# FFN products of 3584 tokens by Strassen's algorithm, with weight sums made once and weights streamed from DRAM

## The chip, the cores and the metric

The kernel runs on one core of a Trainium2 chip. A core has TensorE (matmul), VectorE, ScalarE and GpSimd, which compute on SBUF and PSUM, and SyncE, which here issues the DMAs. The metric is the time on the device in microseconds, as the median of three runs.

## The reference

Block-causal attention (8 batches of 8 heads, 576 positions, 64 wide) gives x; a gated projection with a 5-tap convolution follows; and its result goes through the part that the change touches:

```python
X = np.fft.fft(x, axis=1); X = np.fft.fft(X, axis=2)
u = x + np.real(X).astype(np.float32)
mu = np.mean(u, axis=-1, keepdims=True)
var = np.mean((u - mu) ** 2, axis=-1, keepdims=True)
un = (u - mu) / np.sqrt(var + 1e-06)
ch = np.maximum(un @ w_ch1, 0.0) @ w_ch2      # 512 -> 2048 -> 512
return (u + ch).astype(np.float32)
```

There are 8 x 576 = 4608 tokens. The weights arrive as float64.

## The kernel before

Every float32 product is made of three matmuls on parts of the operands: a high part (the value rounded to the format fp32r) and a low part (what is left): high by high, high by low and low by high. A high part is a copy on ScalarE, a low part a subtraction on VectorE.

phase1() makes attention, gate and the Fourier mix and stores u to DRAM (u_d, one tile for each batch). It ends near 690 us of the trace. XF holds the factors of a head pair; the loads L496 bring some of them back from DRAM. In its last batch first_weights() decodes the weights of hidden blocks 0 and 1 in quarters: a raw load (L891), a decode on ScalarE and VectorE, the high part (L895) and the low part (L896, tiles KP and KL among them).

phase2() is the FFN. The 4608 tokens go in NG = 9 groups of T = 512. A group runs over 16 blocks f of 128 hidden units: 12 matmuls of 512 columns into the PSUM tile psh (L1185 to L1187), relu as the high part hh on ScalarE (L1190), the low part hl on VectorE (L1191), and one block later 12 matmuls into the four sums o (L1204 to L1206). A group is 384 matmuls. At its end VectorE multiplies o by r = 1/sqrt(var) (L1213), GpSimd adds u (L1215; VectorE in the last group), and the rows are stored (L1216). The norm of the next group (norm(), L1139 to L1159) runs in between; its means are matmuls with a matrix of ones (average(), L1121 and L1122). From group 2 on GpSimd makes parts of it. Group 0 also decodes the weights: load_raw (L1082, two DMAs of 0.5 MB for a block, called five blocks ahead, three used up front) and load_w (decode L71 to L82, high part W at L1092, low part W at L1093). The weights of all 16 blocks then stay in SBUF.

A scheduler of the tile framework fixes each engine's order before the run; an engine takes its instructions in that order and waits for semaphores. All DMAs of phase 2 stand in SP's one queue. They take eight semaphores in turn (DMAHW0 to 7), and each waits for the DMA eight before it.

Of the kernel before, what the change touches and what calls it, by code (L numbers as in the profile page):

```python
# [17 lines left out]
def kernel(  # L18
# [13 lines left out]
    nc = tc.nc  # L32
# [61 lines left out]

    cst = ctx.enter_context(tc.tile_pool(name="cst", bufs=1))
# [9 lines left out]
    W1H, W1L, W2H, W2L = ([None] * NF for _ in range(4))  # L105

    def w_places(f, t):
        W1H[f], W1L[f], W2H[f], W2L[f] = (x[:, 0:D] for x in t)

    def w_sources(f):  # L110
        return ((w_ch1[:, f * P:(f + 1) * P].bitcast(I32).rearrange("(c p) f -> p c f", p=P), W1H[f], W1L[f]),
                (w_ch2[f * P:(f + 1) * P, :].bitcast(I32).rearrange("p (c f) -> p c f", c=4), W2H[f], W2L[f]))
# [4 lines left out]
    def phase1():  # L117
        with ExitStack() as c1:
# [766 lines left out]
            def first_weights(z):  # L885

                src, h, l = w_sources(z // 4)[z // 2 % 2]
                hf = z % 2
                h, l = (t[:, 256 * hf:256 * hf + 256] for t in (h, l))
# [3 lines left out]
                st = QHL.rearrange("p t s -> p (t s)")[:, 256 * (z % 4):256 * (z % 4) + 256].bitcast(F32)  # L893
                Chain(wait, wait, wait, wait, *decode(r, st, True),
                      lambda: nc.scalar.copy(out=h, in_=st),  # L895
# [142 lines left out]
    def phase2():  # L1038
        with ExitStack() as c2:
# [11 lines left out]
            NG = NTOK // T  # L1051
            s3 = sb("s3", 2)
            rp = sb("rp", 1)
# [3 lines left out]
            wp = [sb(f"wp{i}", 1) for i in range(2, NF)]  # L1057
            wh = sb("wh", 1)
            wb = sb("wb", 1)
            ps_o, ps_h, ps_t = psum("ps_o", 1), psum("ps_h", 2), psum("ps_t", 2)  # L1060
# [4 lines left out]
            US = [wa.tile([P, 4, T], F32, name="U0")]  # L1065
            UHS = [wa.tile([P, 4, T], F32R, name="UTH0")]
            ULS = [wa.tile([P, 4, T], F32R, name="UTL0")]
            HH = [wa.tile([P, T], F32R, name=f"hh{i}") for i in range(2)]
            HL = [wa.tile([P, T], F32R, name=f"hl{i}") for i in range(2)]
            US.append(wb.tile([P, 4, T], F32, name="U1"))  # L1070
            ULS.append(wb.tile([P, 4, T], F32R, name="UTL1"))

            RAW = {}

            def load_raw(f):

                if not 1 < f < NF:
                    return
                pool = rp if f in (2, NF - 1) else wp[f] if f < NF - 2 else wh
                RAW[f] = pool.tile([P, 4 * D], I32, tag="w", name="rw")  # L1080
                for z, (src, _, _) in enumerate(w_sources(f)):
                    nc.sync.dma_start(out=RAW[f][:, 2 * D * z:2 * D * z + 2 * D].rearrange("p (c f) -> p c f", c=4),  # L1082
                                      in_=src)

            def load_w(f):
                W = wp[f - 2].tile([P, 4 * D], F32R, tag="w", name=f"W{f}")
                w_places(f, [W[:, D * z:D * z + D] for z in (0, 2, 1, 3)])
                h, l = W[:, 0:2 * D], W[:, 2 * D:4 * D]
                st = s3.tile([P, 2 * D], F32, tag="st", name="st")
                for stage in decode(RAW[f], st):  # L1090
                    stage()
                nc.scalar.copy(out=h, in_=st)  # L1092
                nc.vector.tensor_tensor(out=l, in0=st, in1=h.bitcast(F32), op=ALU.subtract)  # L1093

            U, UTH, UTL, RS = {}, {}, {}, {}

            def load_u(g):
                if g >= NG:
                    return
                U[g] = US[g % 2]  # L1100
                done = 0
                while done < T:
                    b, s = divmod(g * T + done, S)
# [210 lines left out]
```

## Time and profile before

| what | value |
|---|---|
| runs | 1474.63, 1480.74, 1481.87 us, median 1480.74 us |
| profiled execution | 1476.05 us, of which the span is 1474.2 us |
| TensorE, VectorE, ScalarE, GpSimd busy | 1420.3, 815.5, 644.5, 309.7 us |
| phase 1, groups 0 and 1, groups 2 to 8 | to about 690 us, to about 850 us, to the end |

The span is the time between the first and the last record of the profiled execution; 1.85 us lie outside it. Busy times are sums over an engine's instructions. The chain of work that ended last is TensorE's for 73% of the span.

### The profile page before, as it was taken

The page shows a single profiled execution, that of the slowest core. Times are in us where ns is not written, and L with a number is a line of the kernel's source. Part 1 is how long each engine was busy: PE and PEld are TensorE (multiplying, and loading weights), DVE is VectorE, ACT ScalarE, POOL GpSimd, SP SyncE. Part 2 cuts the span into 40 slices and gives each one's busy share as a digit, 9 for nine tenths or more (in the row PEclk, how much of TensorE's full clock was granted, in tenths as well). Part 3 has the DMA queues.
Part 4 walks back from the last instruction along what each step waited for, and adds up shares of the span by engine and source line. Part 5 has one row for each costly group of instructions (what it writes and reads, how often), then busy time and mean ns, then how long its engine had stood idle before and what let it go on. Part 6 is the DMA issues. An engine that isn't in the chain of part 4 may idle for free.

```text
span 1474.2 us, 22875 instructions
## 1 busy us (share of the span) xinstructions
PE 1420.3 (96%) x8543; PEld 1205.5 (82%) x8543; DVE 815.5 (55%) x1618; ACT 644.5 (44%) x1627; POOL 309.7 (21%) x254
## 2 busy tenths in 40 slices
PE   5798999999999999999999999999999999999998
PEld 3576888999989898888788888888888888888887
DVE  5777797979797979898983222322232223222212
ACT  5687777777777777734532112121121212112110
POOL 3423232323232323222011011111011111011100
PEclk9799999999999999999999999999999999999999
DMA  7567565656565656353500010100101010010000
GB/s 207 151 161 212 152 179 145 173 148 176 146 177 147 174 150 167 99 175 114 204 29 29 0 57 1 57 0 17 42 0 57 1 53 5 0 58 1 29 0 29
DMA packets 121611, 137.22 MB, mean 93 GB/s; under 512 B 23567, under 2 KB 91421, under 8 KB 121501
## 3 DMA queue, kind: packets, MB, share of 16 engines
q1 hardware_dynamic: 120960, 135.63, 32.2%
q8 instruction: 67, 1.10, 0.3%
q14 instruction: 44, 0.35, 0.1%
q10 hardware_dynamic: 540, 0.14, 0.0%
HBM read 70.57 MB, written 19.01 MB: 61 GB/s over the span
## 4 chain that ended last, share of the span: by engine, by line
PE 73%; DVE 10%; issue 6%; DMA 4%; POOL 3%; ACT 3%; SPq 1%; DVEq 0%; ACTq 0%; POOLq 0%
PE psh L1187 8%; PE psh L1185 8%; PE psh L1186 8%; PE o L1206 8%; PE o L1204 8%; PE o L1205 8%; PE av L605 4%; PE pt L577 4%; DVE gate L632 2%; PE sc L417 2%; POOL XA L838 2%; PE sc L418 2%; PE psx L181 1%; DVE mx L449 1%; PE psx L182 1%
## 5 line engine op out<-in xcount | busy, mean ns | idle before, releaser
L1191 DVE SCALAR_TENSOR_TENSOR hl<-psh,hh 128x512 fp32r<-128x512 f32 x144 | 99.4, 690 | 398.4 <-ACT hh L1190 398.3
L1190 ACT ACTIVATE hh<-psh 128x512 fp32r<-128x512 f32 x144 | 86.1, 598 | 500.2 <-PE psh L1187 500.0
L1187 PE MATMUL psh<-UTH,W 128*128 128x512 f32 x504 | 196.2, 389 | 1.2 <-DVE W L1093 1.2
L1185 PE MATMUL psh<-UTH,W 128*128 128x512 f32 x504 | 196.2, 389 | 1.1 <-ACT W L1092 1.1
L1206 PE MATMUL o<-hl,W 128*128 128x512 f32 x504 | 196.2, 390 | 0.0
L1186 PE MATMUL psh<-UTL,W 128*128 128x512 f32 x504 | 196.1, 389 | 0.0
L1204 PE MATMUL o<-hh,W 128*128 128x512 f32 x504 | 196.1, 389 | 0.0
L1205 PE MATMUL o<-hh,W 128*128 128x512 f32 x504 | 196.0, 389 | 0.0
L463 ACT ACTIVATE PB<-sc,mx 128x128 f32<-128x128 f32 (+4 forms) x320 | 167.0, 527 | 52.8 <-DVE mx L449 29.5
L577 PE MATMUL pt<-ident,PB 128*128 128x128 f32 x800 | 141.9, 283 | 15.4 <-ACT PTb L583 8.1
L577 PEld LDWEIGHTS pt<-ident,PB 128*128 128x128 f32 x800 | 101.0, 144 | 32.5 <-ACT PTb L583 14.5
L632 DVE SCALAR_TENSOR_TENSOR gate<-XF,cw,gate 128x575 f32<-128x575 f32 (+3 forms) x128 | 122.2, 955 | 4.5 <-ACT gate L63 3.6
L1187 PEld LDWEIGHTS psh<-UTH,W 128*128 128x128 f32 x504 | 94.6, 188 | 21.3 <-DVE W L1093 1.6
L1215 POOL TENSOR_TENSOR U<-o,U 128x512 f32<-128x512 f32 x32 | 40.3, 1288 | 341.0 <-DVE o L1213 341.0
L1185 PEld LDWEIGHTS psh<-UTH,W 128*128 128x128 f32 x504 | 94.6, 188 | 21.1 <-ACT W L1092 1.5
L1206 PEld LDWEIGHTS o<-hl,W 128*128 128x128 f32 x504 | 94.5, 188 | 20.6 <-DVE hl L1191 1.0
L1204 PEld LDWEIGHTS o<-hh,W 128*128 128x128 f32 x504 | 94.6, 188 | 19.9 <-ACT hh L1190 0.2
L1205 PEld LDWEIGHTS o<-hh,W 128*128 128x128 f32 x504 | 94.6, 188 | 19.8
L1186 PEld LDWEIGHTS psh<-UTL,W 128*128 128x128 f32 x504 | 94.6, 188 | 19.6
L449 DVE TENSOR_REDUCE mx<-sc 128x1 f32<-128x384 f32 (+2 forms) x192 | 104.3, 560 | 4.4 <-PE sc L183 2.7
L417 PE MATMUL sc<-K,QQ 128*128 128x256 f32 (+2 forms) x256 | 87.9, 354 | 13.4 <-DMA QQ<-QHL 12.5
L628 POOL TENSOR_TENSOR XL<-XF,XH 128x576 fp32r<-128x576 f32 x32 | 45.9, 1434 | 249.3 <-ACT XH L57 249.1
(226 smaller groups left out, 3122.0 us busy)
## 6 DMA issues: line engine op xcount, KB each, us to landing
K<-KP SPq DMA_DIRECT2D x128, 144.0 KB, 2.5
QQ<-QHL SPq DMA_DIRECT2D x128, 128.0 KB, 2.5
rw<-in_w_ch SPq DMA_DIRECT2D x28, 512.0 KB, 7.2
VV<-in_v SPq DMA_DIRECT2D x32, 320.0 KB, 3.6
qraw<-in_q SPq DMA_DIRECT2D x32, 288.0 KB, 3.3
kraw<-in_k SPq DMA_DIRECT2D x32, 288.0 KB, 3.3
out<-U SPq DMA_DIRECT2D x36, 256.0 KB, 2.0
QQ<-QHL SPq DMA_DIRECT2D x128, 64.0 KB, 2.4
```

The source lines that it names most:

```text
L417: nc.tensor.matmul(t[:, o:o + w], q[:, 0, m], KK[p][h][:, 0:w], start=True, stop=False)
L449: nc.vector.reduce_max(out=mx[:, j:j + 1], in_=t, axis=AX.X, negate=one)
L463: nc.scalar.activation(out=PB[i][:, k0:k0 + w], in_=t, func=AF.Exp, bias=nm, accum_out=su[:, at + j:at + j + 1])
L577: nc.tensor.transpose(ps[:, j, :], PB[i][:, (j0 + j) * P:(j0 + j + 1) * P], ident)
L632: nc.vector.scalar_tensor_tensor(out=gate[c][:, s:S], in0=XF[:, 0:S - s], scalar=cw[:, c, 4 - s:5 - s], in1=gate[c][:, s:S], op0=ALU.mult, ...
L1185: nc.tensor.matmul(ps, W1H[f][:, c * P:c * P + P], UTH[g][:, c, :], start=(c == 0), stop=False)
L1186: nc.tensor.matmul(ps, W1H[f][:, c * P:c * P + P], UTL[g][:, c, :], start=False, stop=False)
L1187: nc.tensor.matmul(ps, W1L[f][:, c * P:c * P + P], UTH[g][:, c, :], start=False, stop=(c == 3))
L1191: nc.vector.scalar_tensor_tensor(out=l, in0=ps, scalar=0.0, in1=h.bitcast(F32), op0=ALU.max, op1=ALU.subtract)
L1204: nc.tensor.matmul(po[t], W2H[e][:, c], h, start=(e == 0), stop=False)
L1205: nc.tensor.matmul(po[t], W2L[e][:, c], h, start=False, stop=False)
L1206: nc.tensor.matmul(po[t], W2H[e][:, c], l, start=False, stop=(e == NF - 1))
```

## The change

The first NG = 2 groups are computed as before, with layer 2 two blocks behind layer 1 in place of one, in the same PSUM banks under new names. The other 3584 tokens go in NQ = 4 quads of 896 tokens, two halves of N = 448. Each layer of a quad is a product of 2 x 2 half-blocks by Strassen's algorithm in Winograd's form, seven products in place of eight: the order of the products is L1O and L2O, and a step (g, l, p, i) is a quarter of product p, 12 matmuls of 448 columns. A quad has 56 steps.

- Weights: group 0 stores the decoded weights of each block (w_d, 0.52 MB) and the high and low parts of the blocks that products use unchanged (base_d, 0.79 MB), through SP; first_weights and keep_base do so for blocks 0 and 1. combine() runs in group 1: 16 units that load 0.52 MB from w_d, make four sums on VectorE, split them and store 1.05 MB to comb_d. In the quads every two steps take one chunk of 1.05 MB from base_d or comb_d, in a ring of six SBUF tiles.
- Operands: sums() makes sums of blocks of X or of the hidden blocks h on GpSimd (896 elements a row), operand() the high part on ScalarE and the low part on VectorE, LOOK = 3 steps ahead in a ring of four tiles.
- Results: a product of layer 1 lies in two PSUM banks (a ring of three pairs) and is added into h by VectorE (28 additions a quad, two for each quarter of p = 5), then relu on ScalarE. A product of layer 2 is added to the loaded rows of u (y11, y12, y21, y22) or to e by VectorE, e to y by GpSimd; then the rows are stored.
- norm_x() normalises the next quad's X in place, 448 columns at a time, with sums, squares' sums and half of the scaling on GpSimd.

```diff
+    NH = NF // 2
+    w_d = [dram.tile([P, 2 * D], F32, name=f"w_d{f}") for f in range(NF)]
+    base_d = [[dram.tile([3, P, NH // 2 * D], F32, name=f"base_d{i}{z}") for z in range(2)] for i in range(2)]
+    comb_d = [[dram.tile([4, P, NH // 2 * D], F32, name=f"comb_d{i}{z}") for z in range(2)] for i in range(2)]
...
+                      lambda: (nc.sync.dma_start(out=keep, in_=st), nc.scalar.copy(out=h, in_=st)),
...
-            NG = NTOK // T
+            NG = 2
+            N = 448
+            NQ = (NTOK - NG * T) // (2 * N)
...
+                if f < 2:
+                    for y in range(3):
+                        nc.sync.dma_start(out=to[:, y], in_=WQ[f][y + i].bitcast(F32))
+                    return
...
+                nc.sync.dma_start(out=to, in_=WW[f][:, i * D:i * D + 3 * D].bitcast(F32).rearrange("p (s c) -> p s c", c=D))
...
+                nc.sync.dma_start(out=w_d[f], in_=st)
...
+                def load(k):
+                    if k < len(units):
+                        i, j = units[k]
+                        ins[k] = s3.tile([P, 2, D], F32, tag="st", name="ab")
+                        for z in range(2):
+                            nc.sync.dma_start(out=ins[k][:, z, :], in_=w_d[j + NH * z][:, D * i:D * i + D])
...
+                    t = two[0][:, k % 2]
+                    p = at(("H0", "L0")[k % 2], [P, 4, 2, 256], F32R, "packed")
+                    for z, a, b, op in ((0, a21, a22, ALU.add), (1, t[:, 0], a11, ALU.subtract),
+                                        (2, a11, a21, ALU.subtract), (3, a12, t[:, 1], ALU.subtract)):
+                        nc.vector.tensor_tensor(out=t[:, z], in0=a, in1=b, op=op)
+                    load(k + 2)
+                    nc.scalar.copy(out=p[:, :, 0, :], in_=t)
+                    nc.vector.tensor_tensor(out=p[:, :, 1, :], in0=t, in1=p[:, :, 0, :].bitcast(F32), op=ALU.subtract)
+                    z, jj = divmod(j, NH // 2)
+                    nc.sync.dma_start(out=comb_d[i][z][:, :, jj * D:jj * D + D].rearrange("s p c -> p s c"),
+                                      in_=p.bitcast(F32).rearrange("p s y c -> p s (y c)"))
+                    yield
...
+            L1O, L2O = (1, 6, 2, 7, 5, 3, 4), (1, 3, 5, 2, 6, 7, 4)
+            steps = [(g, l, p, i) for g in range(NQ) for l in range(2) for p in (L1O, L2O)[l] for i in range(4)]
...
+            ring_w = [4, 5, 6, 7, 8, 9]
+            ring_o = [10, 11, 12, 13]
...
+                chunk[c] = at(ring_w[c % 6], [P, 4, 2, 256], F32R, "chunk")
+                src = SRC[l, p][z][SLOT[l, p]] if (l, p) in SRC else comb_d[l][z][SLOT[p]]
+                nc.sync.dma_start(out=chunk[c].bitcast(F32).rearrange("p j y c -> p (j y c)"), in_=src)
...
+                        for t in range(4):
+                            (nc.gpsimd if t % 2 else nc.vector).tensor_tensor(
+                                out=u[:, t, :], in0=u[:, t, :], in1=r, op=ALU.mult)
...
+                x, y, z = {5: (b, b, a), 6: (d, d, b), 7: (a, d, a), 4: (c, d, c)}.get(p, (None,) * 3)
+                if x is not None:
+                    nc.gpsimd.tensor_tensor(out=x, in0=y, in1=z, op=ALU.subtract)
...
+                o = at(ring_o[nitem[0] % 4], [P, 2, 2, N], F32R, "o")
+                nitem[0] += 1
+                nc.scalar.copy(out=o[:, 0], in_=x)
+                nc.vector.tensor_tensor(out=o[:, 1], in0=x, in1=o[:, 0].bitcast(F32), op=ALU.subtract)
...
+                if l == 0:
+                    ps = banks[(k + 2) % 3]
...
+                            nc.tensor.matmul(to, wh, o[:, 0, t], start=(t == 0), stop=False)
+                            nc.tensor.matmul(to, wh, o[:, 1, t], start=False, stop=False)
+                            nc.tensor.matmul(to, wl, o[:, 0, t], start=False, stop=(t == 1))
+                    ps = ps[:, :, 0:N]
+                    a, b, c, d = (hb[z][i // 2][:, i % 2 * 2:i % 2 * 2 + 2] for z in range(4))
+                    if p == 1:
+                        nc.scalar.copy(out=a, in_=ps)
+                        return
+                    for to, x in {6: ((b, a),), 2: ((a, a),), 7: ((c, b),), 5: ((d, c), (b, b)), 3: ((b, b),),
+                                  4: ((c, c),)}[p]:
+                        if p == 4:
+                            nc.vector.tensor_tensor(out=to, in0=x, in1=ps, op=ALU.subtract)
+                        else:
+                            nc.vector.tensor_tensor(out=to, in0=ps, in1=x, op=ALU.add)
...
+                        nc.scalar.activation(out=h, in_=h, func=AF.Relu)
...
+                ps = banks[(k // 4 + 2) % 3]
...
+            LOOK = 3
...
-                for f in range(NF + 1):
+                for f in range(NF + 2):
+                    if g == 0 and f == 0:
+                        for e in range(2):
+                            keep_base(e)
                     if g == 0 and f + 2 < NF:
...
-                    if f == (5 if g else NL):
-                        nxt = norm(g + 1)
+                        keep_base(f + 2)
+                    if g == 0 and f == 9:
+                        load_u(1)
+                    if g == 0 and f == NL:
+                        nxt = norm_g(1)
+                    if g and f == 5:
+                        load_x(0)
+                        nxt = norm_x(0)
+                    if g and 7 <= f < 13:
+                        load_chunk(f - 7)
...
+                for _ in mix:
+                    pass
+                if g == NG - 1:
+                    prepare(3)
...
-                    (nc.vector if g == NG - 1 else nc.gpsimd).tensor_tensor(out=x0, in0=x, in1=x0, op=ALU.add)
+                    nc.gpsimd.tensor_tensor(out=x0, in0=x, in1=x0, op=ALU.add)
...
+                n = k % 56
+                if n == 0:
+                    load_x(g + 1)
+                    nxt = norm_x(g + 1)
+                if k % 2 == 0:
+                    load_chunk(k // 2 + 6 - 1) if k else None
+                if l == 0 and n >= 24:
+                    j = k + 12
+                    src[j + 0] = sums(j)
+                if l and 8 <= n - 28 < 20:
+                    j = k + 8
+                    src[j] = sums(j)
+                if n in (20, 22, 24, 26):
+                    load_y(g, (12, 22, 11, 21)[(n - 20) // 2])
+                prepare(k + LOOK)
+                product(k)
+                if l == 0 or n == 27:
+                    next(nxt, None)
+                if l:
+                    next(nxt, None)
```

SP (the queue of DMAs) at the end of phase 1, before; XF1 holds the last head pair's factors, rw raw weights, and DMAHW, DVE and so on name the semaphores waited for:

```order
L891 DMA rw_8614<-in_w_ch2 128x512 [waits DMAHW7_49,DVE_49,Activation_49]
L891 DMA rw_8616<-in_w_ch2 128x512 [waits DMAHW0_49,DVE_49,Activation_49]
L496 DMA XF1_135<-f_d1_66 64x576 [waits DMAHW4_49,DMAHW3_49,Pool_49]
L496 DMA XF1_135<-f_d1_66 64x512 [waits DMAHW5_49]
L496 DMA XF1_135<-f_d1_66 64x64 [waits DMAHW6_49]
L1082 DMA rw_9286<-in_w_ch1 128x4x256 [waits DVE_49,PE_49]
```

The XF1 loads follow raw loads here.

SP at the same place after; QHL is where the first weights are decoded, K1 and KP are tiles of their high and low parts:

```order
L906 DMA w_d1_68<-QHL_138 128x256
L1177 DMA base_d00_83<-K1_8575 128x512 [waits DMAHW6_49,DVE_49]
L906 DMA w_d1_68<-QHL_138 128x256 [waits DVE_49]
L1177 DMA base_d00_83<-KP_8576 128x512 [waits DMAHW0_49,DVE_49]
L506 DMA XF1_159<-f_d1_66 64x576 [waits DMAHW5_49,DMAHW1_49,Pool_49]
L506 DMA XF1_159<-f_d1_66 64x512 [waits DMAHW2_49]
L506 DMA XF1_159<-f_d1_66 64x64 [waits DMAHW3_49]
```

The XF1 loads now follow stores of w_d and base_d that wait for VectorE.

SP in group 0 just after the last stores of u (u_d7), before; the loads of rw are raw weights:

```order
L843 DMA u_d7_64<-XA_167 128x2x289 [waits DMAHW6_49,DVE_49]
L843 DMA u_d7_64<-XA_167 128x2x289 [waits DMAHW7_49,Activation_49,Pool_49]
L843 DMA u_d7_64<-XA_167 128x2x287 [waits DMAHW0_49,DVE_49]
L843 DMA u_d7_64<-XA_167 128x2x287 [waits DMAHW1_49,Pool_49]
L1082 DMA rw_9359<-in_w_ch1 128x4x256 [waits DMAHW2_49,PE_49]
L1082 DMA rw_9359<-in_w_ch2 128x1024 [waits DMAHW3_49]
L1082 DMA rw_9401<-in_w_ch1 128x4x256 [waits DMAHW4_49,PE_49]
L1082 DMA rw_9401<-in_w_ch2 128x1024 [waits DMAHW5_49]
```

The raw loads stand right behind the stores of u.

SP at the same place after; W4 holds both parts of block 4's weights:

```order
L853 DMA u_d7_64<-XA_191 128x2x289 [waits DMAHW1_49,DVE_49]
L853 DMA u_d7_64<-XA_191 128x2x289 [waits DMAHW2_49,Activation_49,Pool_49]
L853 DMA u_d7_64<-XA_191 128x2x287 [waits DMAHW3_49,DVE_49]
L853 DMA u_d7_64<-XA_191 128x2x287 [waits DMAHW4_49,Pool_49]
L1179 DMA base_d01_84<-W4_9442 128x3x512 [waits DMAHW5_49,DVE_49,Activation_49]
L1167 DMA rw_9408<-in_w_ch1 128x4x256 [waits DMAHW6_49,PE_49]
L1167 DMA rw_9408<-in_w_ch2 128x1024 [waits DMAHW7_49]
L1167 DMA rw_9439<-in_w_ch1 128x4x256 [waits DMAHW0_49,PE_49]
```

A store of W4's parts now stands between the stores of u and the next raw load.

GpSimd in a steady group before (L1149 and L1153 belong to the norm, L1215 adds u):

```order
L1153 TENSOR_TENSOR q_10728<-q_10728,x_10761 128x512 [waits Activation_49]
L1149 TENSOR_TENSOR UTL1_9284<-x_10827,UTH1_9814 128x512 [waits PE_49,Activation_49]
L1153 TENSOR_TENSOR q_10728<-q_10728,x_10794 128x512 [waits Activation_49,Pool_49]
L1153 TENSOR_TENSOR q_10728<-q_10728,x_10827 128x512 [waits Activation_49,Pool_49]
L1215 TENSOR_TENSOR U0_9276<-o_10975,U0_9276 128x512 [waits DMAHW6_49,DVE_49]
L1215 TENSOR_TENSOR U0_9276<-o_10979,U0_9276 128x512 [waits DMAHW7_49,DVE_49]
L1215 TENSOR_TENSOR U0_9276<-o_10983,U0_9276 128x512 [waits DVE_49]
L1215 TENSOR_TENSOR U0_9276<-o_10987,U0_9276 128x512 [waits DVE_49]
```

All are of 512 elements a row, one or two for each step of the norm.

GpSimd in layer 2 of a quad after (L1287 is a sum of hidden blocks, L1371 to L1387 add e to output rows):

```order
L1287 TENSOR_TENSOR h_10774<-h_10774,h_10770 128x896 [waits DVE_49]
L1371 TENSOR_TENSOR y_11248<-y_11248,e_11397 128x448 [waits DMAHW1_49,DMAHW0_49,Activation_49]
L1371 TENSOR_TENSOR y_11251<-y_11251,e_11400 128x448 [waits DMAHW3_49,Activation_49]
L1287 TENSOR_TENSOR h_10768<-h_10774,h_10768 128x896 [waits Pool_49]
L1287 TENSOR_TENSOR h_10774<-h_10774,h_10770 128x896 [waits DVE_49]
L1287 TENSOR_TENSOR h_10768<-h_10774,h_10768 128x896 [waits Pool_49]
L1287 TENSOR_TENSOR h_10771<-h_10773,h_10771 128x896 [waits DVE_49] x2
L1287 TENSOR_TENSOR h_10772<-h_10774,h_10772 128x896 [waits DVE_49] x2
L1384 TENSOR_TENSOR y_11157<-y_11157,e_11397 128x448 [waits DVE_49]
L1384 TENSOR_TENSOR y_11160<-y_11160,e_11400 128x448 [waits DVE_49]
L1384 TENSOR_TENSOR y_11206<-y_11206,e_11397 128x448 [waits DVE_49]
L1387 TENSOR_TENSOR y_11291<-y_11291,e_11397 128x448 [waits DMAHW6_49,DMAHW5_49]
```

In the place of single sums of 512 elements stand sums of 896; those that wait for DVE wait for the low parts that still read the tile.

## Rows read from the trace of the kernel before

**Rows 1.** The page: span; busy us, share and instructions by engine:

```profile
span 1474.2 us, 22875 instructions
...
PE 1420.3 (96%) x8543; PEld 1205.5 (82%) x8543; DVE 815.5 (55%) x1618; ACT 644.5 (44%) x1627; POOL 309.7 (21%) x254
```

**Rows 2.** Stretches: us, busy us of five engines, clock, DMA share, GB/s:

```profile
0.00:700.00 700.00, 653.16 (x5177) 574.37 (x5178) 564.10 (x1298) 491.64 (x1382) 208.93 (x180) 0.98 0.58 160
700.00:760.00 60.00, 57.75 (x253) 47.15 (x252) 59.85 (x73) 31.02 (x39) 0.00 (x0) 1.00 0.36 127
900.00:1400.00 500.00, 499.95 (x2196) 411.74 (x2195) 134.32 (x172) 87.00 (x148) 74.29 (x55) 1.00 0.07 24
694.00:720.00 26.00, 23.75 (x104) 19.05 (x103) 23.68 (x29) 13.61 (x16) 0.00 (x0) 1.00 1.06 375
```

**Rows 3.** Timeline of PE (start, us, line, operation): 51 matmuls, then 22:

```profile
999.82 0.39 PE L1185 MATMUL psh<-UTH,W 128*128 128x512 f32 x1
...
1011.15 0.39 PE L1187 MATMUL psh<-UTH,W 128*128 128x512 f32 x1
...
639.77 0.30 PE L183 MATMUL psv<-XH,wv_l 128*128 128x288 f32 x1
...
642.55 0.29 PE L183 MATMUL psv<-XH,wv_l 128*128 128x288 f32 x1
```

**Rows 4.** Groups by line, weight loads: busy us, mean ns | idle before:

```profile
L1187 PEld LDWEIGHTS psh<-UTH,W 128*128 128x128 f32 x504 | 94.6, 188 | 21.3 <-DVE W L1093 1.6
```

**Rows 5.** Timeline of PE and DVE, the end of the span:

```profile
1469.04 0.39 PE L1206 MATMUL o<-hl,W 128*128 128x512 f32 x1
...
1470.62 0.69 DVE L1215 TENSOR_TENSOR U<-o,U 128x512 f32<-128x512 f32 x1
```

**Rows 6.** Timeline of SP and DVE, end of phase 1; wait in brackets:

```profile
617.57 0.45 SPq L496 DMA_DIRECT2D XF<-f_d  x1
...
619.21 0.42 DVE L896 TENSOR_TENSOR KL<-QHL,KP 128x256 fp32r<-128x256 f32 x1
...
623.49 0.69 DVE L611 TENSOR_TENSOR XF<-av,XF 128x512 f32<-128x512 f32 x1 [1.53 <-PE av L605]
```

**Rows 7.** The chain of waits at the start of group 0 (start us, us, what):

```profile
690.58 5.63 DMA rw<-in_w_ch
...
704.23 1.14 DVE W L1093
```

**Rows 8.** Timeline of DVE: two operations in a row, and one of 1024 columns:

```profile
979.54 0.68 DVE L1191 SCALAR_TENSOR_TENSOR hl<-psh,hh 128x512 fp32r<-128x512 f32 x1
980.14 0.68 DVE L1147 TENSOR_TENSOR x<-U,pm 128x512 f32<-128x512 f32 x1
...
707.62 1.23 DVE L1093 TENSOR_TENSOR W<-st,W 128x1024 fp32r<-128x1024 f32 x1
```

**Rows 9.** Groups by line of ACT, POOL and DVE in phase 2:

```profile
L1190 ACT ACTIVATE hh<-psh 128x512 fp32r<-128x512 f32 x144 | 86.1, 598 | 500.2 <-PE psh L1187 500.0
...
L1215 POOL TENSOR_TENSOR U<-o,U 128x512 f32<-128x512 f32 x32 | 40.3, 1288 | 341.0 <-DVE o L1213 341.0
...
L1159 DVE RECIPROCAL r<-r 128x512 f32<-128x512 f32 x9 | 30.1, 3344 | 0.4 <-ACT r L1158 0.4
```

**Rows 10.** Timeline of DVE and POOL in the norm of a steady group:

```profile
981.33 0.68 DVE L1147 TENSOR_TENSOR x<-U,pm 128x512 f32<-128x512 f32 x1
...
981.55 1.30 POOL L1149 TENSOR_TENSOR UTL<-x,UTH 128x512 fp32r<-128x512 f32 x1 [28.41 <-ACT UTH L1148]
...
983.59 1.29 POOL L1153 TENSOR_TENSOR q<-q,x 128x512 f32<-128x512 f32 x1 [0.74 <-ACT x L1151]
...
984.06 1.37 DVE L1149 TENSOR_TENSOR UTL<-x,UTH 128x512 fp32r<-128x512 f32 x1 [1.45 <-ACT UTH L1148]
...
984.84 1.75 POOL L1149 TENSOR_TENSOR UTL<-x,UTH 128x512 fp32r<-128x512 f32 x1
```

More of the change, by code (lines that the diff above doesn't have):

```diff
@@ L1073, in phase2 @@
[L1073 to L1100, printed above, removed]
-                done = 0
-                while done < T:
-                    b, s = divmod(g * T + done, S)
-                    m = min(T - done, S - s)
-                    nc.sync.dma_start(out=U[g][:, :, done:done + m],
-                                      in_=u_d[b][:, s:s + m].rearrange("(t p) s -> p t s", p=P))
+            banks = [ps_c.tile([P, 2, T], F32, name=f"banks{i}") for i in range(3)]
@@ L1107, in load_u, with tokens, load_rows, average @@
+            def tokens(g):
+                return (g * T, T) if g < 2 * NG else None
+            def load_rows(to, start, n, t0, nt):
+                done = 0
+                while done < n:
+                    b, s = divmod(start + done, S)
+                    m = min(n - done, S - s)
+                    nc.sync.dma_start(out=to[:, :, done:done + m],
+                                      in_=u_d[b][t0 * P:(t0 + nt) * P, s:s + m].rearrange("(t p) s -> p t s", p=P))
                     done += m
-            def average(g, ps, a):
-                if g == 0:
+            def average(ps, a, n, first):
+                if first:
@@ new lines, in phase2, with load_w @@
+            WW = {}
+            def load_w(f):
+                W = at(f, [P, 4 * D], F32R, f"W{f}")
+                WW[f] = W
+                w_places(f, [W[:, D * z:D * z + D] for z in range(4)])
+                h, l = (W.rearrange("p (q y c) -> p q y c", y=2, c=256)[:, :, y] for y in range(2))
+                st = s3.tile([P, 2 * D], F32, tag="st", name="st")
+                for stage in decode(RAW[f], st):
+                    stage()
+                nc.sync.dma_start(out=w_d[f], in_=st)
+                x = st.rearrange("p (q c) -> p q c", c=256)
+                nc.scalar.copy(out=h, in_=x)
+                nc.vector.tensor_tensor(out=l, in0=x, in1=h.bitcast(F32), op=ALU.subtract)
@@ new lines, in phase2, with load_y @@
+            Y = {}
+            def load_y(g, q):
+                col = NG * T + 2 * N * g + N * (q in (12, 22))
+                for m in range(2):
+                    if q == 21 and m == 0:
+                        Y["pair"] = yp.tile([P, 2, N], F32, tag="y", name="y")
+                    Y[q, m] = y = (Y["pair"][:, m] if q == 21 else
+                                   kp.tile([P, S], F32, tag={12: "K0", 22: "K1", 11: "KP"}[q], name="y")[:, 0:N])
+                    load_rows(y.unsqueeze(1), col, N, m + 2 * (q > 20), 1)
```

272 lines of the change are left out of this document (207 added, 65 removed).

## Prediction

> **What bounds the kernel now.** I read first the busy times of the page: TensorE is busy 1420.3 of 1474.2 us, VectorE 55%, GpSimd 21% [rows 1]. Then the table of stretches [rows 2]: phase 1 (0 to 700) keeps three engines busy at once; in 700 to 760, where group 0 decodes its weights, VectorE is busy 59.85 of 60 us and TensorE 57.75; from 900 to 1400 TensorE is busy 499.95 of 500 us at full clock while VectorE has 134, GpSimd 74 and the DMA engines a share of 0.07. So in groups 2 to 8 nothing but the matmuls sets the time, and the other engines and the DMA have room. The change trades in that room: fewer columns for TensorE, more work for all others.
>
> **The matmuls.** The number does not change: seven groups had 7 x 384 = 2688 matmuls of 512 columns, the quads have 224 steps x 12 = 2688 of 448 columns. In a steady stream 512-column matmuls start (1011.15 - 999.82) / 50 = 226.6 ns apart, 288-column ones (642.55 - 639.77) / 21 = 132.4 ns [rows 3]. The slope is 0.4205 ns a column, so 448 columns take 226.6 - 64 x 0.4205 = 199.7 ns. Gain: 2688 x 26.9 ns = **-72.3 us**. In proportion to the columns it would be 198.3 ns (-76.0 us). A weight load shows as 188 ns [rows 4], which would leave no more than this; that it does not set the pace is shown by the 288-column rows, 132 ns apart with a load each. The matmuls of the norms (34 before, 38 after) cost nothing worth a term.
>
> **The tail.** Now the last matmul starts at 1469.04, VectorE's last add at 1470.62 and the span ends at 1474.2 [rows 1, 5]: 5.2 us. After, one subtraction from PSUM and a smaller store follow the last matmul, without the product by r. **-1.4 us.**
>
> **End of phase 1.** The loads of XF (the last head pair's factors) go at 617.57 on SP. In the new order they stand behind the copies w_d and base_d of the first weights, which wait for VectorE's low parts; the last of those begins at 619.21. VectorE's use of XF at 623.49 waited 1.53 us for TensorE [rows 6], which is the slack. A delay of 619.6 - 617.6 plus the stores' turn is 2 to 4 us against 1.5: **+2** (0 to +4).
>
> **Group 0.** VectorE is the bound there and its own work hardly changes. But its decode begins with a raw load: the chain shows 5.63 us of DMA for it from 690.58 and VectorE's low part at 704.23 [rows 7]. In the new order the base_d copy of W4, 0.79 MB, stands before that load. At 375 GB/s, what 694 to 720 moved [rows 2], that is 2.1 us. From then on each block moves raw 1.05 + base_d 0.79 + w_d 0.52 = 2.36 MB, 6.3 us, where VectorE needs some 5.7 for a block; the raws run three blocks ahead, so only a part of 10 x 0.6 us shows. **+5** (+2 to +12).
>
> **Group 1.** It has 384 matmuls, 87 us. Moved meanwhile: 16 units of sums at 1.57 MB, six chunks, the first X, rows of u and outputs, some 35.2 MB, 94 us at 375 GB/s; the last two stores need not be done by its end. VectorE has 16 x (4 x 0.42 + 1.14) = 45 us for the sums besides its low parts and fits. **+4** (0 to +12). The Trainium skill's page "HBM Reference", Specifications (TRN2), gives about 358 GB/s for a core whose neighbour streams and about 425 for one alone: 98 or 83 us for this stretch, the total then 4 us more or 4 us less. The stretch of the trace lies between, and decides.
>
> **The quads.** A quad is 56 x 12 = 672 matmuls, 134.2 us, 2.40 us a step, 67.1 us a layer.
> *Weights.* 28 chunks and the X, Y and output rows are 34.9 MB a quad: 260 GB/s against 375. A chunk is asked for ten steps (24 us) ahead, so I cost the stream at nothing; its cover is that lead, and without it see the third rival.
> *Layer 1.* VectorE operations that follow each other start 0.60 us apart at 512 columns (979.54 to 980.14) and last 1.23 at 1024 [rows 8], so about 1.0 us for 896. It has 28 additions of products (28 us), 7 low parts (7), and the next quad's norm: 20 operations of some 0.53 and two reciprocals of 3.34 x 448/512 = 2.9 [rows 9], 16 us. 51 of 67 us: hidden.
> *Layer 2.* GpSimd took 1.288 us for 512 columns [rows 9], so 2.25 for 896 and 1.13 for 448. In this half it has 12 sums (27 us), 8 additions (9) and some 7 for the next quad's first sums; VectorE has 28 low parts (28 us) and 14 additions from PSUM. The trace shows that an operation of VectorE with both inputs in SBUF and one of GpSimd do not run together: the low part at 984.06 took 1.37 us while GpSimd was in its sum from 983.59, and GpSimd's own next took 1.75. The subtraction at 981.33, with one input in PSUM, kept 0.68 beside GpSimd's from 981.55 [rows 10]. So low parts and sums add up: 28 + 27 + 9 + 7 = 71 us for 67.1 us of matmuls. In the 12 steps with a sum, VectorE gets one low part per 1.0 + 2.25 = 3.25 us, TensorE uses one per 2.40: 12 x 0.85 = 10.2 us short, of which the lead of three operands covers 7.2. That leaves 3 us a quad, 12 in all. ScalarE's high part, 598 ns at 512 columns [rows 9], about 1.05 at 896, fits in a step.
> *Entries.* Three quads begin with two GpSimd sums in a row (4.5 us) that have to be done three steps (7.2 us) on, with ScalarE and VectorE behind them (2 us); a GpSimd backlog over 0.7 us shows, one addition of 2.25 at most likely: 3 x 1.3 = 4. The first quad's norm ends in group 1, where TensorE waits for its sum of squares once: 2. Together **+18** (0 to +45; the upper end is a GpSimd that is always behind: no lead, 10 a quad).
>
> **Sum**, against the profiled 1476.05 us (span 1474.2 and 1.85 around it): 1476.05 - 72.3 - 1.4 + 2 + 5 + 4 + 18 = 1431.4. The profiled run lies 0.3% under the median 1480.74, inside the three runs; I say **1432**.
>
> **Rivals.**
> *Hardly a stall* (1400 to 1413): the leads swallow the shared port, and group 0 and 1 stay at their lower ends: 1476 - 72.3 - 1.4 + 2 + 2 + 0 + 0 = 1406. For it: sums are called eight steps before their use, and GpSimd was busy 15% in steady groups [rows 2]. Against: 71 us of exclusive work in 67.
> *The port binds* (1450 to 1475). If GpSimd starts each layer 2 with a backlog, the lead is spent at once: 10.2 a quad, and the p=6 and p=7 sums late as well, 16 x 0.85 = 14 a quad, 54 in all: 1431 - 18 + 54 = 1467. For it: the two stretched rows, 1.37 and 1.75 us [rows 10]. The Trainium skill, "SBUF — State Buffer", Who interferes with whom, has this as a rule: the pair is held by one of the two for a whole instruction, and which of them began first decides who waits; the trace agrees with 1.37 for 0.68 us.
> *The stream binds* (slower): chunks, X, Y and stores go through SP's one queue in order, and each DMA waits for the eighth before it. Stalls begin under 260 GB/s; the gain is gone when a quad takes 16 us more, under 34.9 MB / 150 us = 233 GB/s. At 200 GB/s a quad takes 174.5 us: 1413 + 4 x 40 = 1573. For it: phase 1 moves 160 GB/s only. Against: it does that at a share of 0.58, so 276 at a full one, and 375 was seen [rows 2].
> *The matmuls don't get shorter*: if 448 columns cost the same 226.6 ns, the -72.3 is gone: 1504. Against: the 288-column rows [rows 3].
>
> **How the numbers follow.** Forecast, 10 to 45 us of new stalls (1413 to 1450): 0.66. Hardly a stall: 0.13. The port: 0.12. The stream: 0.06. No shorter matmuls: 0.03. The range for 8 in 10 takes the forecast and most of its two neighbours: 1408 to 1465. A measurement of this kernel tells apart some 0.5%, 7.4 us: faster is under 1473.3, slower over 1488.1. Faster: 0.66 + 0.13 + 0.08 of the port's; same: 0.04 of the port's and 0.01 of the stream's; slower: the rest. 0.87, 0.05, 0.08.
>
> **What would show it.** Matmul rows of 448 columns 200 ns apart; TensorE busy near 67 us a layer and idle mostly in layer 2, put down to VectorE's low part or ScalarE's high part of o, in the second half of each; GpSimd near 80% there; 250 to 260 GB/s in the quads with no wait for a chunk. Group 0 ends about 9 us later than now, group 1 lasts 88 to 95 us. Wrong would be: waits for chunks, a granted clock under 1 in the quads because of stalls, idle time in layer 1 over 3 us a quad, or a phase 1 that moved by more than 4 us.

## The result, and the profile after

The changed kernel takes 1487.72 us (median of 10 runs) against 1479.84 us of the kernel before on the same chips: 1.0061 times as long, 95% interval 1.0043 to 1.0078. It was forecast at 1432, faster. The profiled execution took 1490.79 us, with a span of 1489.0. The page of the kernel after, with its span, the busy times, and the three groups of instructions that matter most (busy us, mean ns | idle before):

```profile
span 1489.0 us, 24090 instructions
...
PE 1385.4 (93%) x8547; PEld 1215.6 (82%) x8547; DVE 1184.9 (80%) x1873; ACT 786.8 (53%) x1738; POOL 539.1 (36%) x348
...
L1304 DVE TENSOR_TENSOR o<-h,o 128x896 fp32r<-128x896 f32 x112 | 208.3, 1888 | 30.8 <-ACT o L1303 30.8
L1287 POOL TENSOR_TENSOR h<-h 128x896 f32<-128x896 f32 x64 | 168.3, 2643 | 95.9 <-ACT h L1349 62.9
...
L1346 DVE TENSOR_TENSOR h<-banks,h 128x896 f32<-128x896 f32 x96 | 102.4, 1082 | 39.8 <-PE banks L1335 39.8
```

Against [rows 1] TensorE is busy 35 us less, but idle twice as long. VectorE went from 55 to 80%, GpSimd from 21 to 36%. The low parts of operands (L1304) last 1.89 us each where 1.0 was put in the sum, GpSimd's sums (L1287) 2.64 for 2.25; the additions that read PSUM (L1346) keep 1.08.

Where the time lies is read from four positions on TensorE: the last matmul of phase 1, the first of group 0, the first of the quads and the last of all. The kernel after:

```profile
679.07 0.29 PE L842 MATMUL pss<-dft,YC 128*128 128x290 f32 x1
...
679.65 0.79 PE L1432 MATMUL banks<-UTH,K 128*128 128x512 f32 x1
...
883.21 0.36 PE L1333 MATMUL banks<-o,chunk 128*128 128x448 f32 x1
...
1484.41 0.36 PE L1361 MATMUL banks<-o,chunk 128*128 128x448 f32 x1
```

The kernel before, the first matmul of group 0 and of group 2:

```profile
664.99 0.40 PE L1185 MATMUL psh<-UTH,K 128*128 128x512 f32 x1
...
851.57 0.39 PE L1185 MATMUL psh<-UTH,K 128*128 128x512 f32 x1
```

Group 0 begins 14.7 us later. The quads begin at 883.21 where group 2 began at 851.57: **31.6 us lost** before the first quad. The quads take 601.4 us, the seven groups in their place took 617.7 (both from the first matmul to the last, [rows 5] for before, and the last counted at the spacing of its stream): **16.3 us gained** where 54 were forecast. The tail gives 0.5. Sum +14.8, the difference of the spans.

The stretches of the kernel after (columns as in [rows 2]): groups 0 and 1, layer 1 and layer 2 of the first quad, layer 2 of the second, layer 1 of the last:

```profile
680.00:780.00 100.00, 92.17 (x388) 72.77 (x387) 84.53 (x98) 38.70 (x50) 5.74 (x4) 0.97 0.81 285
780.00:883.00 103.00, 94.42 (x395) 74.82 (x394) 80.19 (x113) 33.74 (x47) 24.89 (x18) 0.97 0.83 298
883.00:970.00 87.00, 74.28 (x346) 65.75 (x345) 75.82 (x70) 33.61 (x42) 41.28 (x24) 0.96 0.66 241
970.00:1047.00 77.00, 71.35 (x338) 64.57 (x337) 62.64 (x46) 29.04 (x33) 51.02 (x24) 0.96 0.70 241
1123.00:1196.00 73.00, 70.66 (x337) 64.40 (x338) 64.36 (x45) 30.39 (x34) 50.71 (x22) 0.98 0.64 219
1344.00:1413.00 69.00, 69.00 (x335) 62.66 (x335) 39.92 (x37) 24.18 (x26) 11.26 (x6) 1.00 0.67 240
```

Undisturbed steps take 2.43 us, so a layer 68.0. The eight layers took 87.0, 76.8, 76.5, 72.3, 74.4, 73.8, 69.4 and 71.2: 57 us over. The one layer with little GpSimd work, layer 1 of the last quad (11 of 69 us, no norm beside it), loses 1.4, and that is a slower cadence of its matmuls, not a wait (last section).

In the first quad the granted clock is down to 0.96. In the quads it fell five times to 0.50, the lower level of 1.2 GHz, for 3 to 7 us, each time during or just after a wait of TensorE of 1.4 to 5.5 us. One such stretch:

```profile
904.20:908.60 4.40, 4.40 (x13) 3.93 (x13) 0.71 (x1) 0.46 (x1) 0.00 (x0) 0.50 1.00 316
```

Matmuls start 0.37 us apart there, for 0.20 at full clock; over the five stretches that costs 8.6 us. The waits of TensorE in the quads (us in total, times, longest):

```profile
PE banks L1360 <- DVE o L1304: 12.2, 10, 5.2
PE pv L1107 <- ACT ah L1104: 6.0, 4, 1.6
PE banks L1333 <- ACT h L1339: 5.5, 1, 5.5
```

and what stands behind them, VectorE and GpSimd in a stretch of layer 2 (two, two and six operations run together into one row):

```profile
1152.37 5.95 DVE L1304 TENSOR_TENSOR o<-h,o 128x896 fp32r<-128x896 f32 x2
...
1160.37 5.89 DVE L1304 TENSOR_TENSOR o<-h,o 128x896 fp32r<-128x896 f32 x2
...
1151.45 16.78 POOL L1287 TENSOR_TENSOR h<-h 128x896 f32<-128x896 f32 x6
```

Low parts and sums alternate without a gap: 5.95 us for two low parts that need 1.07 each alone, 16.78 for six sums that need 2.07. One of each takes some 2.9 us, and TensorE wants a low part every 2.43.

The longest wait of layer 2 is of another kind. TensorE, then VectorE and GpSimd before it:

```profile
993.10 0.74 PE L1360 MATMUL banks<-o,chunk 128*128 128x448 f32 x1 [5.18 <-DVE o L1304]
...
988.63 2.48 DVE L1116 TENSOR_TENSOR s<-s,s 128x448 f32<-128x448 f32 x1 [5.29 <-POOL s L1115]
...
980.00 7.50 POOL L1287 TENSOR_TENSOR h<-h 128x896 f32<-128x896 f32 x3
987.46 1.13 POOL L1115 TENSOR_TENSOR s<-X 128x448 f32<-128x448 f32 x1
```

VectorE stood idle for 5.29 us: in its order a step of the next quad's norm (L1116) stood ahead of the low part, and it waited for a sum of GpSimd (L1115) that stood behind three operand sums.

### The profile page after: what moved, and what is told of

Read it like the earlier page. It is cut to its first block, busy times and chain, and to the rows that moved or that the text cites. A ratio compares the mean times of both kernels' runs of the same rounds, so it can differ in the third digit from the quotient of the medians.

```text
span 1489.0 us, 24090 instructions
## 1 busy us (share of the span) xinstructions
PE 1385.4 (93%) x8547; PEld 1215.6 (82%) x8547; DVE 1184.9 (80%) x1873; ACT 786.8 (53%) x1738; POOL 539.1 (36%) x348
## 5 line engine op out<-in xcount | busy, mean ns | idle before, releaser
L1304 DVE TENSOR_TENSOR o<-h,o 128x896 fp32r<-128x896 f32 x112 | 208.3, 1888 | 30.8 <-ACT o L1303 30.8
L1287 POOL TENSOR_TENSOR h<-h 128x896 f32<-128x896 f32 x64 | 168.3, 2643 | 95.9 <-ACT h L1349 62.9
L1303 ACT CAST o<-h 128x896 fp32r<-128x896 f32 x112 | 105.4, 943 | 171.0 <-PE banks L1361 131.3
L1360 PE MATMUL banks<-o,chunk 128*128 128x448 f32 x448 | 167.2, 373 | 12.2 <-DVE o L1304 12.2
L1333 PE MATMUL banks<-o,chunk 128*128 128x448 f32 x448 | 166.3, 371 | 6.3 <-ACT h L1339 5.5
L1359 PE MATMUL banks<-o,chunk 128*128 128x448 f32 x448 | 166.0, 371 | 2.9 <-DVE h L1344 2.9
L1334 PE MATMUL banks<-o,chunk 128*128 128x448 f32 x448 | 166.1, 371 | 1.5 <-DVE o L1304 1.5
L1361 PE MATMUL banks<-o,chunk 128*128 128x448 f32 x448 | 166.0, 371 | 0.0
L1335 PE MATMUL banks<-o,chunk 128*128 128x448 f32 x448 | 165.9, 370 | 0.0
L1346 DVE TENSOR_TENSOR h<-banks,h 128x896 f32<-128x896 f32 x96 | 102.4, 1082 | 39.8 <-PE banks L1335 39.8
L587 PEld LDWEIGHTS pt<-ident,PB 128*128 128x128 f32 x800 | 101.0, 144 | 32.0 <-ACT PTb L593 14.7
L1360 PEld LDWEIGHTS banks<-o,chunk 128*128 128x128 f32 x448 | 85.5, 191 | 23.4 <-DVE o L1304 16.1
L1349 ACT ACTIVATE h<-h 128x896 f32<-128x896 f32 x64 | 60.8, 952 | 74.8 <-DVE h L1346 50.7
L1333 PEld LDWEIGHTS banks<-o,chunk 128*128 128x128 f32 x448 | 85.2, 190 | 15.2 <-ACT h L1339 5.9
L593 ACT COPY PTb<-pt 128x512 f32<-128x512 f32 (+1 forms) x160 | 86.8, 546 | 18.9 <-PE pt L587 18.2
L1359 PEld LDWEIGHTS banks<-o,chunk 128*128 128x128 f32 x448 | 85.6, 191 | 10.8 <-DVE h L1344 3.3
```

Source lines behind the costliest of these rows:

```text
L587: nc.tensor.transpose(ps[:, j, :], PB[i][:, (j0 + j) * P:(j0 + j + 1) * P], ident)
L1287: nc.gpsimd.tensor_tensor(out=x, in0=y, in1=z, op=ALU.subtract)
L1304: nc.vector.tensor_tensor(out=o[:, 1], in0=x, in1=o[:, 0].bitcast(F32), op=ALU.subtract)
L1333: nc.tensor.matmul(to, wh, o[:, 0, t], start=(t == 0), stop=False)
L1334: nc.tensor.matmul(to, wh, o[:, 1, t], start=False, stop=False)
L1335: nc.tensor.matmul(to, wl, o[:, 0, t], start=False, stop=(t == 1))
```

## The experiments

Totals are medians; the kernel before took 1478.7 to 1479.5 beside them. Four theories were at stake: VectorE and GpSimd holding each other up, the order at the end of phase 1, the transfers of groups 0 and 1, and the weight stream.

**All GpSimd work of the quads on VectorE** (the shared access against VectorE's own load):

```diff
-                    nc.gpsimd.tensor_tensor(out=x, in0=y, in1=z, op=ALU.subtract)
+                    nc.vector.tensor_tensor(out=x, in0=y, in1=z, op=ALU.subtract)
```
(and so for the sums of X, the norm's parts, the scaling and the additions of e)

> The change with all GpSimd work of the quads (operand sums, parts of the norm, additions of e) on VectorE; nothing is left out. In the changed kernel the quads take 601 us (883.2 to 1484.6) where 224 steps at their undisturbed 2.43 us would take 544: 57 us of stalls. Theory (VectorE and GpSimd hold each other up on SBUF): without GpSimd the low part of 896 columns falls from 1.89 us to 1.08, layer 2 loses its stalls (22 us over the four quads), layer 1 is filled to some 67 of 68 us by VectorE alone and keeps a part of its 35: total 1455 to 1465 us. Rival (VectorE's own load is the limit, it is busy 80% already): no gain or a loss, 1485 to 1520 us.

Measured 1438.69 us, 0.9725 of before (0.9711 to 0.9740): 49 us gained by using one engine less. The page's span, the low parts and the stretch of layer 2 of the first quad:

```profile
span 1436.8 us, 24005 instructions
...
L1304 DVE TENSOR_TENSOR o<-h,o 128x896 fp32r<-128x896 f32 x112 | 120.8, 1089 | 25.2 <-ACT o L1303 24.6
...
950.00:1019.00 69.00, 68.32 (x335) 62.81 (x336) 64.41 (x77) 30.15 (x34) 0.00 (x0) 1.00 0.77 263
```

The low part is down from 1.89 to 1.09 us, TensorE is idle for 0.7 of 69 us where it was idle for 5.6 of 77, and layer 2 takes 69.1, 68.1, 68.1 and 68.1. The granted clock in the quads is 1.00 for 0.98. VectorE's total hardly changed (1172.1 for 1184.9 us): what it took over, it had spent waiting. The theory holds, and its size was underestimated: I had expected layer 1 to stay full. Not all of the gain lies in the quads, which take 558.3 us for 601.4: they also begin 9.0 us sooner (874.23). The edit moves the norm of the first quad too, which runs in group 1 beside the weight sums; 2 of the 9 come from an earlier start of group 0 (677.56), which the edit doesn't touch. The edit ends the sharing and also changes the engine: a sum of hidden blocks takes 1.09 us on VectorE and 2.07 at best on GpSimd. That sharing counts is shown by the low parts, which the edit leaves as they were; how much of the 49 us is GpSimd's own speed was not separated.

**The sums left out** (the operands are then wrong; measures the sums alone):

```diff
-                if x is not None:
-                    nc.gpsimd.tensor_tensor(out=x, in0=y, in1=z, op=ALU.subtract)
```
(and the sums of X)

> The change without the sums of operands on GpSimd (20 sums of 896 columns a quad are left out; products take the blocks as they are). Theory (the shared access of VectorE and GpSimd): the low parts run at 1.1 us in layer 2, the stalls of layer 2 go (22 us) and the first quad's wait for its first sums (8 us), total 1450 to 1462 us. Rival (the stalls come from the norm of the next quad and from the transfers): under 10 us, 1478 to 1487 us.

Measured 1444.39 us (0.9766). 43 us, 6 more than the theory's range: yet leaving the sums out is worth less than moving all GpSimd work, so the norm's parts and the additions of e had a share too.

**The sums alone on VectorE** (only the five lines of sums() moved):

> The change with the operand sums alone on VectorE; the norm's parts and the additions of e stay on GpSimd. All of GpSimd's work moved was worth 49 us. Theory (what counts is the time GpSimd holds the access: the sums are 207 of its some 300 us in the quads, and long ones hold a low part up longest): 1488 - 35 to 42 = 1446 to 1453 us. Rival (the norm's chain is what is late, its short operations wait for low parts): over half of the 49 us stay, 1463 us or more.

Measured 1451.37 us (0.9817; 0.9789 to 0.9845): 36 of the 49 us, as the theory said. Layer 2 took 68.1 us in all four quads.

**The weight stream left out** after six chunks (the products take wrong weights):

```diff
+                if c >= 6:
+                    chunk[c] = chunk[c - 6]
+                    return
```

> The change without the weight stream in the quads: only the first six chunks are loaded, all later steps use these six again (106 MB less moved). Theory: the chunks are there in time and nothing changes, 1484 to 1489 us. Rival (the transfers slow the quads, by late chunks or late rows behind them in SP's queue): quads nearer to 544 us, total 1450 us or less.

Measured 1480.92 us (1.0012; 0.9998 to 1.0027): 7 us, give or take 3, for 106 chunks (111 MB). The stream is not the main cause, but its share is a little more than the theory allowed.

**No weight preparation** (no w_d, base_d, no sums of weights; chunks of the same bytes from u, so the products are of other data):

> The change without the weight copies w_d and base_d and without the weight sums (combine); the quads' chunks are loaded from u in DRAM, the same bytes. In the changed kernel the quads begin at 883 us, group 2 of the kernel before began 31 to 33 us sooner. Theory (transfers and VectorE work of the preparation take these 33 us, and two late units of the sums another 8 in the first quad): quads begin at 852 to 858 us, total 1445 to 1457 us. Rival (the new order on TensorE at the end of phase 1 takes some 10 to 13 of them whatever is stored): quads begin at 865 us or later, total 1460 us or more.

Measured 1460.05 us (0.9870; 0.9837 to 0.9903). The quads began at 867.25: 16 us of the 31.6 are the preparation's, and 15.7 stay with none of it. Group 0 still began at 679.05. The trace speaks for the rival, something else in the order. The totals don't decide: they scatter from 1454.51 to 1464.80, over both ranges, and the trace is of the slowest. The next run tests the order directly.

**One-bank PSUM tiles in the first two groups.** The change had put these groups' sums into the quads' tiles of two banks:

```diff
-                po = [banks[t // 2][:, t % 2] for t in range(4)]
+                po = [ps_o.tile([P, D], F32, tag=f"o{t}", name=f"o{t}") for t in range(4)]
...
-                        ps = banks[2][:, f % 2]
+                        ps = ps_h.tile([P, T], F32, tag="h", name="psh")
```
(the pool of banks is opened behind group 1)

> The change with the first two groups in PSUM tiles of one bank each, as before the change (four for o, two for psh, the pair for the norm at the same place), and the three tiles of two banks only from the quads on. In the changed kernel group 0's first matmul stands behind all of phase 1 (679.65 us; 664.99 in the kernel before, between matmuls of the last transform); without the weight preparation it still stood at 679.05 and the quads began at 867 us, not at 852. Theory (a tile of two banks is the unit that is waited for, and moves the group's first products behind the transform): quads begin 11 to 15 us sooner than 883, total 1470 to 1477 us. Rival (group 0 is held by VectorE's decode and the transfers anyway, so an earlier start is lost again): quads begin less than 4 us sooner, total 1483 to 1488 us.

Measured 1471.27 us (0.9942; 0.9921 to 0.9964). TensorE of this kernel at the start of group 0 and of the quads:

```profile
666.03 0.28 PE L809 MATMUL psy<-dft,XSP 128*33 128x258 f32 x1
666.15 0.39 PE L1435 MATMUL psh<-UTH,K 128*128 128x512 f32 x1
...
871.12 0.36 PE L1336 MATMUL banks<-o,chunk 128*128 128x448 f32 x1
```

Group 0's first product stands between the transform's matmuls again (666.15), the quads begin 12.1 us sooner. No wait was removed by hand: with a tile of two banks the scheduler put the group's matmuls behind all of phase 1, with one-bank tiles into its gaps. Why it did so, the runs don't show; the edit changes the size of the tiles and the place where the pool of banks is opened, and the two were not separated. Of the 13.5 us by which group 0 begins sooner, 3.7 are an earlier end of phase 1 in this execution (its last matmul at 675.33 for 679.07).

**Both edits together:**

> Both edits together: no GpSimd work in the quads, and one-bank PSUM tiles in the first two groups. Theory (the two causes lie in different stretches and add): 1438.7 - 13 = 1426 us (1423 to 1430). Rival (the earlier start is eaten in group 0): 1435 to 1440 us.

Measured 1437.54 us (0.9721): 1 us, not 12. The rival holds: the quads began 6 us sooner (868.19 for 874.23), and their first layer took 80.1 us for 76.0. So the gains of the two causes don't add up.

**The weight sums sooner**, on top of both:

```diff
-                    if f:
+                    for _ in range(min(f, 2) if f < 8 else 1):
                         next(mix, None)
```

> As e6, with the weight sums made sooner: two of the 16 units at each of the blocks 2 to 7 of group 1 in place of one. With all GpSimd work on VectorE the first quad's layer 1 still took 76 us for 68, since the last units of the weight sums stand among its first operands. Theory: the first quad loses 2 us in place of 8, total 1418 to 1422 us. Rival (group 1 is at the limit of the transfers, 411 GB/s at 820 to 840, so units can't be made sooner): no gain or a few us lost, 1424 to 1432 us.

Measured 1433.99 us (0.9695). That is above both ranges, which were set from the forecast of the run before, not from what it measured; against that run it is 3.6 us gained, where the theory had 6 and the rival none. The first layer took 72.3 us for 80.1, but the quads began 3.6 us later. In group 0 a block now takes 7.4 us for 5.44 of matmuls.

**No base_d**, on top of this (products take other weights):

> As e7, without the stores base_d (12.6 MB in group 0); the chunks that came from there are loaded from comb_d instead, so the products take other weights. The earlier start of group 0 (665 for 680 us) brought the quads only 3 to 6 us, and group 0 now advances 7.4 us a block where its matmuls take 5.44. Theory (group 0 goes at the pace of its transfers, 2.36 MB a block): with 1.57 MB a block it goes at 5.5 to 5.8 us, the quads begin 10 to 14 us sooner, total 1420 to 1424 us. Rival (VectorE's decode sets the pace, or the raw loads that stand in SP's queue behind stores which wait for VectorE): the quads begin less than 4 us sooner, total 1430 to 1434 us.

Measured 1421.77 us (0.9616; 0.9597 to 0.9636), quads from 861.39 for 871.82. A stretch of group 0 with base_d, then without (columns as in [rows 2]):

```profile
726.00:748.00 22.00, 18.71 (x72) 12.82 (x72) 16.35 (x19) 7.80 (x9) 0.00 (x0) 1.00 0.97 335
```

```profile
726.00:748.00 22.00, 21.92 (x94) 16.80 (x94) 21.46 (x26) 10.33 (x13) 0.00 (x0) 1.00 0.48 170
```

With fewer bytes TensorE goes from 18.71 to 21.92 of 22 us, and VectorE's decode goes faster too: group 0 had been held by its transfers, at 335 GB/s and a share of 0.97. In the second of these stretches the raw loads are nearly over, which is why so little is moved; in 702 to 726, where both kernels still load, it is 375 and 318 GB/s, with TensorE busy 22.21 and 24.00 of 24 us. Blocks 8 to 14 go at 6.1 us where they went at 7.6, not at the 5.5 to 5.8 of the theory; VectorE is now busy 21.46 of 22 us. The edit also takes away the wait of the raw loads behind stores that wait for VectorE. The next run speaks for the bytes: it keeps the base_d stores in their place and stores no w_d from block 8 on, and its blocks 8 to 14 go at 5.5 us.

**Half of w_d** (for eight blocks the sums take high + low part from SBUF):

```diff
-                nc.sync.dma_start(out=w_d[f], in_=st)
+                if f < NH:
+                    nc.sync.dma_start(out=w_d[f], in_=st)
...
+                        nc.vector.tensor_tensor(out=ins[k][:, 1, :].rearrange("p (q c) -> p q c", c=256),
+                                                in0=x[:, :, 0], in1=x[:, :, 1], op=ALU.add)
```

> As e7, but w_d is stored for the first eight blocks only; of the other eight the sums take high part + low part from the weights in SBUF (one more addition of 512 columns on VectorE for each of the 16 units). 8.4 MB less moved in groups 0 and 1, 22 us at 375 GB/s; VectorE has 16 x 0.6 = 10 us more in group 1. Theory (the transfers bound groups 0 and 1): 4 to 9 us gained, total 1425 to 1430 us. Rival (VectorE is as full there): no gain, 1433 to 1440 us.

Measured 1434.68 us (0.9696): nothing. Group 0 ended 10 us sooner; group 1, with VectorE full, gave back 7 of them (the quads began at 868.56 for 871.82), and the first layer of the quads the rest (78.2 us for 72.3).

**The same addition on GpSimd:**

> As e10, with the added operation (high part + low part, 512 columns, both inputs in SBUF) on GpSimd instead of VectorE. e10 left group 0 some 10 us sooner than e7 and lost it again in group 1, where VectorE was full. Theory (an operation of GpSimd holds VectorE's two-input operations up for its whole 1.29 us, longer than VectorE's own 0.6): no better than e10, 1433 to 1440 us. Rival (GpSimd is idle there and takes 10 us of work away from VectorE): 1424 to 1429 us.

Measured 1423.73 us, 0.9628 of before (0.9613 to 0.9642): the rival holds, and this is the fastest kernel that computes the whole. Group 1 and the first steps of the quads with the addition on VectorE, then on GpSimd, with GpSimd's row:

```profile
774.00:874.00 100.00, 91.58 (x391) 73.86 (x392) 93.94 (x156) 35.36 (x48) 8.76 (x6) 0.97 0.88 311
```

```profile
774.00:874.00 100.00, 93.94 (x412) 76.23 (x411) 91.45 (x139) 35.82 (x50) 29.10 (x21) 1.00 0.88 311
...
L1214 POOL TENSOR_TENSOR ab<-W 128x512 f32<-128x512 f32 x16 | 23.0, 1440 | 123.9 <-DVE W L1198 71.1 <-DVE two L1226 40.1 <-issue 12.7
```

Sixteen operations of 1.44 us (1.29 alone) beside a VectorE at 91%: the two do collide a little, but VectorE is rid of an operation each time, and its low parts of the weight sums stay near their length (1.26 us for 1.22). What decides how much collides was not tried. The quads began 2.4 us sooner, and their first layer took 71.1 us for 78.2.

**Norm and additions of e back on GpSimd**, on top of the earlier weight sums:

> As e7, but the norm's parts and the additions of e go back to GpSimd; only the operand sums stay on VectorE. With the sums alone moved, layer 2 of all four quads took 68.1 us, without a stall; layer 1 lost 2 to 3 us in each quad with a norm. Theory (short operations of GpSimd cost little where VectorE has slack, and more in group 1, where it has none): 1433 to 1438 us. Rival (VectorE relieved of some 14 us a quad): 1426 to 1431 us.

Measured 1442.03 us (0.9745; 0.9728 to 0.9761), 8 us more than without. The direction is the theory's, the loss larger than its range: the first layer took 77.5 us for 72.3, and four layers went at a slower cadence of matmuls (below).

## Why the prediction was wrong

*The matmuls.* -72.3 at 199.7 ns each; undisturbed steps of 2.43 us make it 202.5 ns and -64.8. The straight line through 288 and 512 columns was 2.8 ns off.

*The quads' stalls.* This is the step that failed most: +18 forecast, against 57.1 us over the undisturbed pace, or 48.5 beyond the 8.6 that the seven groups also had over theirs (617.7 - 2688 x 0.2266). Of the 57, matmuls of the norm are 4.9 and 104 steps at the slower cadence 5.2. The other 47 are stalls: 31.4 us of idle TensorE, 8.6 us of matmuls at the lower clock behind its waits, and 7 us that I can't assign. The price of a collision was near: 3.25 us a pair forecast, 2.9 measured. Two things were wrong with its use. Layer 1 was called hidden, 51 of 67 us, by adding up VectorE alone; but its chain (norm on GpSimd and ScalarE, sums, low parts) passes the shared access several times, and it lost 35 us where 6 were put in. Not all of this is the shared access: with no GpSimd work in the quads 12.6 of the 35 us stay, 8.0 of them in the first quad, where the longest wait of all (5.49 us, TensorE at 903.90) ends when ScalarE can copy into a tile of h that the last weight sums had held (rp). That these run into the quads was put at nothing. And in layer 2 the lead of three operands was credited in full (22 us lost, 12 forecast), and no term was put in for VectorE standing behind GpSimd's queue (5.29 us at 988.63). A busy share says nothing of a chain that passes from engine to engine. The rival *the port binds* had the mechanism; it got 0.12 because I took the lead for a cover. That its 54 us are close to the 57 is luck: it put all of them into layer 2, which lost 22. Two of the signs of being wrong came: a granted clock under 1 in the quads, and idle time over 3 us in layer 1 (12.7 and 4.4 us in the first two quads). The Trainium skill's "SBUF — State Buffer", Who interferes with whom, states the rule behind the collisions, an exclusive hold of a shared pair of ports; the trace agrees, with low parts between 1.07 and 3.02 us.

*The end of phase 1.* VectorE's use of XF came 1.7 us later (625.18 for 623.49, [rows 6]), and +2 was forecast, but that is luck: the same operation one batch before, ahead of the new stores, was already 2.5 us later (551.31 for 548.77), and in five experiments with the same phase 1 it lay between 621.33 and 625.17. No run shows a cost of the XF loads. And the step looked at SP's order alone. TensorE's order had changed too: group 0 began 14.7 us later. With one-bank PSUM tiles it began 13.5 us sooner again, some 10 of them by its new place in the order and the rest by the end of phase 1. I had read that order for no term of the sum.

*Groups 0 and 1.* +9 forecast. The preparation costs 16 (no-preparation run). The bytes were right; but the two groups were costed apart, with raw loads said to run ahead. They stand in SP's queue behind the stores, so group 0 went at the pace of its bytes as soon as nothing else held it. The two stretches of the changed kernel moved 285 and 298 GB/s on the mean; shorter ones came near the 375 of [rows 2] or passed it: 370 in 700 to 730, 397 in 820 to 840, and 411 in 820 to 840 with all GpSimd work on VectorE. The Trainium skill's "HBM Reference", Specifications (TRN2), has about 358 for a core beside a streaming neighbour and about 425 for one alone; the trace lies on both sides of the first, and no stretch looked at reached the second. The GpSimd work of the first quad's norm, in group 1, has a share too (some 7 us). The 16, the 10 of the tiles and these 7 are not parts of a sum: the edits for the last two together brought the quads 15.0 us sooner (868.19 for 883.21).

*The stream.* Costed at nothing, worth some 7 us; the rival that gave the slower side to it had the wrong mechanism.

*The sum, as it came out*, against the span before: -64.8 of matmuls, +48.5 in the quads, +31.6 before them, -0.5 at the end (-1.4 forecast): +14.8. The result lay in none of the cases I had priced (the port alone gave 1467) because the stalls of that rival came together with 31.6 us before the quads, where +11 was forecast, and one cause of these, the order of TensorE, was on no list.

## What to carry to other kernels

Before trading matmul time for work on VectorE and GpSimd, add up what both do with two inputs in SBUF, and follow the chain, not the busy shares: here the same work on VectorE alone was 49 us faster. GpSimd paid in one place, 16 short operations beside a full VectorE (11 us); as a second VectorE in the quads it didn't, and giving it the short operations back cost 8. When tiles are renamed or regrouped, read the order of the engine that sets the time at the seam, and sum the bytes of neighbouring stages together.

## What was not expected of the hardware

Matmuls of 448 columns keep one of two cadences. Layer 1 of the last quad, first matmul and first of the next layer, in the kernel after:

```profile
1344.02 0.37 PE L1333 MATMUL banks<-o,chunk 128*128 128x448 f32 x1
...
1413.46 0.37 PE L1359 MATMUL banks<-o,chunk 128*128 128x448 f32 x1
```

and in the kernel with all sums on VectorE:

```profile
1296.29 0.37 PE L1333 MATMUL banks<-o,chunk 128*128 128x448 f32 x1
...
1364.38 0.36 PE L1359 MATMUL banks<-o,chunk 128*128 128x448 f32 x1
```

336 matmuls each, the same work at full clock: 69.44 and 68.09 us, 206.7 and 202.6 ns. In the changed kernel the cadence changes only after a stall and then stays until the next; 104 undisturbed steps of the changed kernel went at the slower one, 90 at the faster. What sets it is open.
